# Pooled attention and a two-layer block on one core: the left-over keys of batch 0 used first, w1's first quarter in two loads, k of batch 1 and w2's second quarter ahead of q of batch 1

## The chip, the cores and the metric

The kernel runs on one core of one Trainium2 chip. The metric is the device time of one execution in microseconds (us), taken as the median of the runs. The core has five engines with a queue each: TensorE (PE, with its weight loads shown apart as PEld), VectorE (DVE), ScalarE (ACT), GpSimd (POOL) and SyncE (SP). Each queue runs in order, and DMAs are issued from SP's, ACT's and POOL's queues. A DMA issued from POOL can change the type of the data; here it turns float32 into 16 bits.

## What is computed

```python
batch, n_heads, seq, head_dim = (8, 8, 576, 64)      # q, k, v, float32
n_tokens, d_model, d_ff = (4608, 512, 2048)

k_p = k.reshape(B, H, 72, 8, D).mean(axis=3)         # keys and values averaged by eights
v_p = v.reshape(B, H, 72, 8, D).mean(axis=3)
scores = scale * q @ k_p^T
attn = exp(scores - max) / sum(exp(scores - max))
x = (attn @ v_p), heads side by side                 # 4608 x 512
h = x @ w_in                                         # w_in 512 x 2048, "w1" below
g = h - tanh(h)
out = g @ w_out                                      # w_out 2048 x 512, "w2" below
```

## The kernel before

The order of the work is written out by hand: within each engine's queue the instructions run in the order in which the code issues them, and semaphores that the framework derives from the tiles are all that holds one engine for another. The DMAs issued from POOL share eight semaphores in turn, so each of them also waits until the one eight places before it has landed; those of SP and ACT together share another eight in the same way.

**Batch by batch.** Batch b's 512 first query rows per head and its 64 last ones (the tail) are handled apart. Groups g = 0 to 8 are the two-layer block: groups 0 to 7 take the 512 first rows of a batch, group 8 collects all the tails. Group g's products run on PE while the other engines prepare batch g + 1. Group 0 is special: its output products (`mlp_o`, L625) go in four passes (quarters 0, 8, 4, 12 of w2's sixteen row blocks, `W2_ORDER`), for four blocks of 128 rows each; `mlp_o(0, tb, qd)` is row block tb with pass qd, four products of 512 columns. Later groups use a form with seven half products (L709) on sums and differences of w2's quarters, which `w_sum` (L695) builds into `w2s` during group 0 (`sum0` to `sum3`, `negated`).

**Tiles of keys.** The 8 heads have 72 pooled keys each, 576 rows. Two heads make 144 rows, of which 128 go into a main tile (four of them, t = 0 to 3) and 16 are left over; the left-overs of the four pairs (64 rows) make a fifth tile, NM. `load_main` loads main tiles, `load_dense` the left-over rows in one DMA, `load_left` in four. `pool_k` adds eights in three steps (8 to 4, 4 to 2, 2 to 1) and writes the result twice into `kd`; PE turns it (`turn_tile`); `kb_main` and `kb_left` copy it from PSUM into the layout `KB`. Scores of a main tile are one product of 512 columns, those of the left-overs four products on 32 rows each (`score_mms`), each followed by ACT's Exp. For batch 0, v is loaded as 16 bits into `v_bf` and pooled on PE with eight products (`v_pe_pool`, L900); the left-over v rows come as float32 and are cast by POOL (L862), and are then spread to their places by PE with the matrix `spread`. `v_main` and `v_left` multiply by a mask into `VB`. `av_pair` forms attn @ v with the sums in an extra column, divides (L954, L955) and `x0_turn` turns the result for `h_part`, the first products with w1 (L602).

**The start.** SP loads k of batch 0 (tiles 0, 1, then 2 and 3), ACT loads q of batch 0 in three parts, then the left-over keys and the left-over v rows. POOL makes the identity and the mask, loads v of batch 0, w1 in four quarters of 512 columns (`load_w1`, L783), w2's first quarter, casts the left-over v, loads q of batch 1 (tail L863, rest L864, in 16 bits, into unused parts of `w2s`), w2's second quarter, clears some tiles, loads v of batch 1 tiles 0 and 1 and w2's third quarter. SP's load of k of batch 1 (`load_k(1)`, L875) is tied to the landing of w1's second quarter. PE fills waits with `warm_pe`, products on zeros whose result is not used.

**Batch 1 in group 0.** `pool_k(1, nc.gpsimd, last=nc.vector)` (L1043) does the first addition on POOL (L268) and the other two on DVE, with `q1_reorder` (L254, two DVE copies from `q1_bf` to `q_bf`) between these. PE's order (L1044 to L1070): four blocks of `mlp_o` pass 0, q's transposes for head pairs 0 and 1, the keys' transposes, `mlp_o` block 0 of pass 1, the other q transposes and the tail, scores of tiles 0 and 1, block 1 of pass 1, the remaining scores, then five more blocks. Batch 2's loads on SP (L1072) are tied to the landing of w2's third quarter.

**PSUM.** Eight banks of 128 x 512 float32. `ps_any` hands them out: during batch 0's attention alternately from (5, 6, 7) and (0, 1, 2), later (`ps_b1`) in turn from (4, 5, 6, 7). The hidden tile i > 5 of group 0 uses bank i % 5; `mlp_o` blocks 0 to 3 collect in banks 1, 2, 3, 0.

Of the kernel before, what the change touches and what calls it, by code (L numbers as in the profile page):

```python
# [8 lines left out]
FP32 = mybir.dt.float32  # L9
# [20 lines left out]
NT = 5  # L30
# [4 lines left out]
NM = 4  # L35
# [8 lines left out]
def kernel(  # L44
# [9 lines left out]
    nc = tc.nc  # L54
# [28 lines left out]
    ps_h = Banks(0, 1, 2)  # L83
# [48 lines left out]
    q_raws = {}  # L132
    rot = [0]

    def ps_any(shape, dtype, name):
        pool, tag = [(ps_a, "ps_a"), (ps_h, "hT_ps")][rot[0] % 2]
        rot[0] += 1
        return pool.tile(shape, dtype, name=name, tag=tag)

# [9 lines left out]
    def load_main(src, dst, b, t0, t1, eng=nc.sync):  # L149
        return eng.dma_start(out=dst[:, t0:t1, :], in_=src[b, 0:128, t0:t1, :])  # L150
# [7 lines left out]
    def load_dense(src, dst, b, eng=nc.sync):  # L158
        return eng.dma_start(
            out=dst[0 : NM * LO, NM, :], in_=src[b, 128:PR, :, :]  # L160
        )
# [92 lines left out]
    def q1_reorder():  # L254
        for h in (0, 4):
            nc.vector.tensor_copy(
                out=q_bf[:, 0:R, h : h + 4, :].rearrange("p j h d -> p h j d"),
                in_=q1_bf[:, h : h + 4, :, :],
            )

    def pool_k(b, eng, t0=0, t1=NT, last=None, dep=None):
# [16 lines left out]
        )  # L278
        if b == 1:
            q1_reorder()  # L280
        kd_done = (last or eng).tensor_tensor(
# [495 lines left out]
    zeros = xT_last[:, 3, :, :].rearrange("p f c -> p (f c)")  # L777
    w1_dmas = []
    w2_dmas = []

    def load_w1(c):
        w1_dmas.append(
            nc.gpsimd.dma_start(  # L783
                out=w1b[:, :, c * 512 : (c + 1) * 512], in_=w1_src[:, :, c * 512 : (c + 1) * 512]
            )
        )

    def load_w2(i, n):
        w2_dmas.append(
            nc.gpsimd.dma_start(out=w2b[:, i : i + n, :], in_=w2_src[:, i : i + n, :])  # L790
        )
# [31 lines left out]
    load_q0(4, 8)  # L823
    load_dense(k_pairs, k_raw[0], 0, nc.scalar)
    load_dense(v_pairs, v_raw[1], 0, nc.scalar)
# [32 lines left out]
    )  # L858
    for c in range(4):
        load_w1(c)  # L860
    load_w2(0, 4)
    nc.gpsimd.tensor_copy(out=v_bf[:, NM, :], in_=v_raw[1][:, NM, :])  # L862
    nc.gpsimd.dma_start(out=q1_tail[:QT], in_=q[1, :, QA:S, :].rearrange("h p d -> p h d"))  # L863
    nc.gpsimd.dma_start(  # L864
        out=q1_bf, in_=q[1, :, 0:QA, :].rearrange("h (p j) d -> p h j d", j=R)
    )
    load_w2(8, 4)
    nc.gpsimd.memset(w2s[64:128, 3, 6:8, :], 0.0)
    nc.gpsimd.memset(k_raw[1][:, NM, :], 0.0)
    nc.gpsimd.memset(v_raw[0][:, NM, :], 0.0)  # L870
    nc.gpsimd.memset(KB[1][:, :], 0.0)
    load_main(v_pairs, v_raw[1], 1, 0, 2, nc.gpsimd)
    load_w2(4, 4)

    after(load_k(1), w1_dmas[1])  # L875

# [5 lines left out]

    def k_turn_left():
        ps = ps_any([128, 128], FP32, "kT_ps")
        turn_tile(ps[:, :], kdups[0], NM)
        kb_left(KB[0], ps, nc.vector.tensor_copy)

    pool_k(0, nc.vector, 0, 1)
# [34 lines left out]
    q_turn(nc.scalar.copy, 6, 8)  # L923
    pool_k(0, nc.vector, 2, 4)
    warm_pe(6)
    k_turn(2, 4)
    pool_k(0, nc.vector, NM, NT)
    warm_pe(2)
    q_pe_transpose(0, (2, 3), "act")
    vs0 = v_pe_pool(0, 2, ident, 4)  # L930
    v_main(VB[0], vs0, nc.vector, 0, 2)
    warm_pe(1, b0=3)
    scores_wide(0, (2, 3))
    v_ps = v_pe_pool(NM, NT, spread)
    k_turn_left()
    v_left(VB[0], v_ps[:, 0, :, :], nc.vector)
    warm_pe(1, b0=3)
    scores_wide(0, (NM,))
    vs1 = v_pe_pool(2, 4, ident, 3)
    v_main(VB[0], vs1, nc.vector, 2, 4)  # L940
    load_left(v_pairs, v_raw[1], 1, nc.scalar)
    pool_v1(NM, NT, nc.gpsimd)
    v1_last = load_main(v_pairs, v_raw[1], 1, 2, 4, nc.gpsimd)
    load_w2(12, 4)
    gts = []
# [38 lines left out]

    av_pair(0, 0, 1, (0, 1))
    av_pair(1, 0, 6, (0, 1))
    av_pair(0, 0, 1, (2,))
    av_pair(1, 0, 6, (2,))
    av_pair(0, 1, 3)
# [23 lines left out]
    for i in range(5, NHID):  # L1013
        mlp_h(0, i, gts, bank(i % 5 if i > 5 else 5, [128, TG]))
        if i == 7:
            q_pe_tail(0)
        if i == 9:
            scores_tail(0)
        if i == 11:
            ps_a.n = 0  # L1020
            av(0, 4, ps_any, True)
    def turn1(blk):
        x_pe_transpose(1, blk, x_pairs[1, blk // 2][:, blk % 2])
# [18 lines left out]

    pool_k(1, nc.gpsimd, last=nc.vector)  # L1043
    mlp_o(0, 0, 0, gts)  # L1044
    mlp_o(0, 1, 0, gts)
    mlp_o(0, 2, 0, gts)
    mlp_o(0, 3, 0, gts)
    q_pe_transpose(1, (0, 1), "act")
    k_transpose(1, ps_any, (nc.vector.tensor_copy, nc.vector.tensor_copy))
    sum1(0)  # L1050
    mlp_o(0, 0, 1, gts)
    q_pe_transpose(1, (2, 3), "act")
    q_pe_tail(1)
    sum2(0)
    sum0(0)
    pool_v1(0, 2)
    scores_wide(1, (0, 1))
    mlp_o(0, 1, 1, gts)
    scores_wide(1, (2, 3))
# [5 lines left out]
    sum0(4)  # L1065
    mlp_o(0, 2, 1, gts)
    mlp_o(0, 3, 1, gts)
    mlp_o(0, 0, 2, gts)
# [143 lines left out]
```

## Time and profile before

| | |
|---|---|
| median of 8 runs | 283.18 us (282.71 to 283.28) |
| the profiled execution | 283.22 us, its span 281.3 us |
| mean granted PE clock | 0.999 |
| DMA by queue (share of 16 engines' span) | SP 33.87 MB (47.9%), POOL 13.77 MB (19.9%), ACT 1.84 MB (2.2%) |
| first product with w1 (L602) | 16.27 us |
| first `mlp_o` (L631) | 31.54 us |
| first product of group 1 (L644) | 51.63 us |

The loads that matter here, from the view of DMA issues (start of the issue, us to landing):

| load | queue | issued | to landing |
|---|---|---|---|
| k batch 0 tiles 2, 3 (512 KB) | SP | 1.74 | 6.0 |
| left-over keys of batch 0 (128 KB) | ACT | 2.38 | 7.1 |
| left-over v of batch 0 (128 KB) | ACT | 3.07 | 7.2 |
| v batch 0 tiles 0, 1 (256 KB in 16 bits) | POOL | 3.70 | 7.0 |
| w1 first quarter (512 KB in 16 bits) | POOL | 5.96 | 9.2 |
| w1 fourth quarter | POOL | 8.17 | 18.3 |
| w2 first quarter | POOL | 8.90 | 21.2 |
| q tail of batch 1 | POOL | 11.27 | 19.3 |
| q of batch 1 | POOL | 11.97 | 21.3 |
| w2 second quarter | POOL | 12.85 | 23.2 |
| v batch 1 tiles 0, 1 | POOL | 15.73 | 21.6 |
| k batch 1 (1024 KB), then its left-overs | SP | about 18.4, 19.03 | 9.5, 9.8 |
| w2 third quarter | POOL | 18.83 | 21.0 |
| v batch 1 tiles 2, 3 | POOL | 22.49 | 18.6 |
| w2 fourth quarter | POOL | 26.72 | 16.8 |

The landings of w1's second and third quarter follow from the medians of neighbouring issues: about 18.5 and 21.9 us.

How to read the lines below: a line of a view in order of time has the start in us, the duration in us, the engine, the line of the code, the operation, what it writes and reads, and in brackets how long the engine was idle before and what released it. A line of the stretches has the stretch, its length, the busy us of PE, PEld, DVE, ACT and POOL (with the number of instructions), the granted PE clock, the share of the DMA engines and the GB/s. The durations of PE's products are modelled and overlap: a product of 512 columns shows 0.38 us, while twenty in a row take 4.31 us.

### The profile page before, as it was taken

Reading aid. Unit: us, or ns where it says so; the run is one execution under the profiler, and the core shown is the slowest. Engines: PE = TensorE matmul, PEld = TensorE weight load, DVE = VectorE, ACT = ScalarE, POOL = GpSimd, SP = SyncE. Lnnn points to the kernel's source line nnn. Section 1 sums busy time; section 2 is a strip of 40 time slices with the busy share of each in tenths; the row PEclk is TensorE's granted clock in tenths of the full one; section 3 lists DMA queues with packets and bytes.
Section 4 is the critical chain, followed back from the end, with each engine's and each line's share of the span. In section 5 each row is a group of like instructions: output and inputs, shape, how many; then the busy total and the mean of one; then the engine's idle time right before and its main releaser. Section 6 shows DMA issues by size and latency. Waiting matters only on the chain.

```text
span 281.3 us, 5492 instructions
## 1 busy us (share of the span) xinstructions
PE 273.6 (97%) x2172; PEld 180.8 (64%) x2174; DVE 221.5 (79%) x336; ACT 155.0 (55%) x209; POOL 116.4 (41%) x131
## 2 busy tenths in 40 slices
PE   7999999999999999999999999999999999999993
PEld 2574455446984598458845894589448954884683
DVE  6758988689948995799679976998599749927982
ACT  4757383777337734774376537662857156126510
POOL 8853401991695059604970398029901100010000
PEclk9999999999999999999999999999999999999999
DMA  7999999989858894879598969796730430021014
GB/s 246 241 212 277 229 261 349 250 178 304 222 99 228 255 274 80 222 248 293 91 193 252 321 88 153 233 349 116 161 117 1 86 149 2 0 89 64 0 41 111
DMA packets 66491, 49.82 MB, mean 177 GB/s; under 512 B 42104, under 2 KB 55944, under 8 KB 66466
## 3 DMA queue, kind: packets, MB, share of 16 engines
q1 hardware_dynamic: 55538, 33.87, 47.9%
q0 software_dynamic: 8736, 13.77, 19.9%
q10 hardware_dynamic: 2192, 1.84, 2.2%
q8 instruction: 17, 0.28, 0.5%
q14 instruction: 8, 0.07, 0.1%
HBM read 36.70 MB, written 9.44 MB: 164 GB/s over the span
## 4 chain that ended last, share of the span: by engine, by line
PE 85%; DMA 10%; DVE 1%; POOL 1%; SPq 0%; ACT 0%; issue 0%
PE PS L644 39%; PE PS L713 35%; DMA w2b<-in_moe_w_out_dram 8%; PE PS L631 4%; PE PS L483 3%; PE PS L457 3%; DMA k_raw<-in_k_dram 2%; PE PS L498 1%; PE PS L409 0%; PE PS L580 0%; POOL v_raw L862 0%; POOL w2s L864 0%; SPq L150 0%; DVE k_raw L268 0%; POOL w2s L863 0%; ACT qT L144 0%
## 5 line engine op out<-in xcount | busy, mean ns | idle before, releaser
L644 PE MATMUL PS<-xT,w1b 128*128 128x512 bf16 (+1 forms) x504 | 98.0, 355 | 0.0
L670 DVE TENSOR_TENSOR Gt<-PS,TS 128x1024 bf16<-128x1024 f32 x56 | 68.3, 1222 | 33.7 <-ACT TS L669 33.6
L644 PEld LDWEIGHTS <-w1b 128*128 128x128 f16 x576 | 56.3, 98 | 52.8
L669 ACT ACTIVATE TS<-PS 128x1024 f32<-128x1024 f32 x56 | 57.3, 1024 | 29.7 <-PE PS L644 27.4
L757 POOL TENSOR_TENSOR m<-O,m 128x512 f32<-128x512 f32 x6 | 7.6, 1259 | 75.1 <-ACT m L755 53.5
L713 PE MATMUL PS<-w2s,Dg 128*128 128x256 f16 x256 | 30.2, 273 | 0.0
L268 POOL TENSOR_TENSOR k_raw<-k_raw 128x512 f32<-128x512 f32 (+2 forms) x13 | 21.1, 1635 | 17.7 <-DVE w2s L696 16.3
L478 ACT ACTIVATE E<-PS 72x1024 bf16<-72x1024 f32 (+1 forms) x30 | 26.1, 929 | 3.9 <-PE PS L457 3.7
L713 PEld LDWEIGHTS <-Gt 128*128 128x128 bf16 x256 | 23.6, 98 | 6.9 <-issue 2.4
L713 PEld LDWEIGHTS <-P 128*128 128x128 bf16 x256 | 24.6, 98 | 3.0
L713 PEld LDWEIGHTS <-Dg 128*128 128x128 bf16 x256 | 24.6, 98 | 2.8
L678 DVE TENSOR_TENSOR P<-Gt 128x1024 bf16<-128x1024 bf16 (+1 forms) x31 | 22.0, 708 | 0.5
L764 ACT COPY m<-PS 128x512 f32<-128x512 f32 x8 | 4.7, 586 | 29.6 <-PE PS L713 29.6
L729 POOL DMA_DIRECT2D out_dram<-O x14 | 7.7, 553 | 31.6 <-DVE O L767 29.5
L688 DVE TENSOR_TENSOR Dg<-Gt 128x1024 bf16<-128x1024 bf16 x32 | 20.4, 685 | 0.0
L534 DVE TENSOR_TENSOR x_sb<-PS,rden 128x512 bf16<-128x512 f32 x28 | 19.4, 692 | 1.0
L293 POOL TENSOR_TENSOR v_raw<-v_raw 128x512 f32<-128x512 f32 (+1 forms) x12 | 18.7, 1575 | 0.0
L713 PE MATMUL PS<-w2s,Gt 128*128 128x256 f16 x128 | 16.4, 273 | 0.0
L713 PE MATMUL PS<-w2b,P 128*128 128x256 f16 x128 | 16.3, 273 | 0.0
L713 PE MATMUL PS<-w2b,Gt 128*128 128x256 f16 x128 | 16.3, 272 | 0.0
L713 PE MATMUL PS<-w2s,Q 128*128 128x256 f16 x128 | 16.3, 272 | 0.0
L1174 ACT COPY O<-PS 128x512 f32<-128x512 f32 x7 | 4.1, 585 | 21.9 <-PE PS L713 21.9
(124 smaller groups left out, 396.3 us busy)
## 6 DMA issues: line engine op xcount, KB each, us to landing
k_raw<-in_k_dram SPq DMA_DIRECT2D x7, 1024.0 KB, 6.0
out_dram<-O POOLq DMA_DIRECT2D x14, 512.0 KB, 4.7
v_raw<-in_v_dram SPq DMA_DIRECT2D x6, 1024.0 KB, 8.1
q_raw<-in_q_dram SPq DMA_DIRECT2D x6, 1024.0 KB, 11.3
w1b<-in_moe_w_in_dram POOLq DMA_DIRECT2D x4, 512.0 KB, 13.1
w2b<-in_moe_w_out_dram POOLq DMA_DIRECT2D x4, 512.0 KB, 21.1
v_raw<-in_v_dram POOLq DMA_DIRECT2D x2, 512.0 KB, 20.1
out_dram<-O SPq DMA_DIRECT2D x2, 512.0 KB, 6.5
```

Of the source, the lines that this page charges most:

```text
L268: first = eng.tensor_tensor(out=r[:, ta:tb, 0:4, :], in0=r[:, ta:tb, 0:4, :], in1=r[:, ta:tb, 4:8, :], op=ALU.add,)
L293: eng.tensor_tensor(out=r[:, ta:tb, 0:4, :], in0=r[:, ta:tb, 0:4, :], in1=r[:, ta:tb, 4:8, :], op=ALU.add,)
L457: nc.tensor.matmul(dst, lhsT=kv[a * D : (a + 1) * D, m, :], rhs=rhs, start=True, stop=True,)
L478: nc.scalar.activation(out=e, in_=ps, func=ACT.Exp, scale=SCALE)
L534: nc.vector.tensor_tensor(out=x_sb[:, :, :, :], in0=ps[:, :, :, 0:D], in1=rden[:, :, :, :].to_broadcast([128, 2, 4, D]), op=ALU.mult,)
L631: nc.tensor.matmul(o_ps[:, :], lhsT=gts[i][:, tb * 128 : (tb + 1) * 128], rhs=w2b[:, i, :], start=(i == 0), stop=(i == NHID - 1),)
L644: nc.tensor.matmul(dst[:, t0 * 128 : t1 * 128], lhsT=w1b[:, fb, i * 128 : (i + 1) * 128], rhs=x[:, t0:t1, fb, :], start=(fb == 0), stop=(f ...
L669: nc.scalar.activation(out=t2, in_=PS[:, b0 : b0 + 2, :], func=ACT.Tanh)
L670: nc.vector.tensor_sub(out=Gt[:, p, :, :], in0=PS[:, b0 : b0 + 2, :], in1=t2)
L678: nc.vector.tensor_tensor(out=P[:, a:b, :], in0=Gt[:, a:b, 0, :], in1=Gt[:, a:b, 1, :], op=ALU.add)
L688: return nc.vector.tensor_tensor(out=Dg[:, a:b, :, :], in0=Gt[:, a:b, :, 0:HT], in1=Gt[:, a:b, :, HT:TG], op=ALU.subtract,)
L713: nc.tensor.matmul(part(g, bk, tt), lhsT=lhs(k, slice(tt * 128, (tt + 1) * 128)), rhs=rhs[:, k, :], start=(first and k == 0 and (tt == 0 o ...
```

## The change

- The left-over keys of batch 0 are loaded on SP behind the main tiles, not on ACT. They are pooled, turned (`k_turn_left(3)`) and scored ahead of tiles 2 and 3. Their warm-up product goes, the banks of batch 0's attention are written out, and `av_pair` takes its three parts in one go.
- w1's first quarter is loaded as two halves of 256 columns.
- k of batch 1 is loaded from POOL's queue, behind w1, not from SP's with a tie. Behind it come w2's first and second quarter, then q of batch 1; then the batch 1 left-over v (its four small loads are issued by SP, not ACT), v tiles 0 and 1, w2's third quarter, and, inside the loop over hidden tiles (before tile 15 is issued), batch 1's `pool_k`, v tiles 2 and 3 and w2's fourth quarter.
- In batch 1 the keys' transposes come ahead of the fourth block of pass 0; `sum1(0)` and `q1_reorder` follow, two blocks of pass 1, all q transposes, and the scores lie between the last two blocks of pass 1.

```diff
@@ pool_k
-        if b == 1:
-            q1_reorder()
@@
-    def load_w1(c):
...
+    def load_w1(c0, c1):
+        nc.gpsimd.dma_start(out=w1b[:, :, c0:c1], in_=w1_src[:, :, c0:c1])
@@
-    load_dense(k_pairs, k_raw[0], 0, nc.scalar)
+    load_dense(k_pairs, k_raw[0], 0)
     load_dense(v_pairs, v_raw[1], 0, nc.scalar)
@@
-    for c in range(4):
-        load_w1(c)
+    for c0, c1 in ((0, 256), (256, 512), (512, 1024), (1024, 1536), (1536, 2048)):
+        load_w1(c0, c1)
+    load_main(k_pairs, k_raw[1], 1, 0, NM, nc.gpsimd)
+    nc.gpsimd.tensor_copy(out=v_bf[:, NM, :], in_=v_raw[1][:, NM, :])
+    nc.gpsimd.memset(k_raw[1][:, NM, :], 0.0)
+    load_dense(k_pairs, k_raw[1], 1, nc.gpsimd)
     load_w2(0, 4)
-    nc.gpsimd.tensor_copy(out=v_bf[:, NM, :], in_=v_raw[1][:, NM, :])
+    nc.gpsimd.memset(w2s[64:128, 3, 6:8, :], 0.0)
+    load_w2(8, 4)
     nc.gpsimd.dma_start(out=q1_tail[:QT], in_=q[1, :, QA:S, :].rearrange("h p d -> p h d"))
+    nc.gpsimd.memset(v_raw[0][:, NM, :], 0.0)
+    nc.gpsimd.memset(KB[1][:, :], 0.0)
     nc.gpsimd.dma_start(
         out=q1_bf, in_=q[1, :, 0:QA, :].rearrange("h (p j) d -> p h j d", j=R)
     )
-    load_w2(8, 4)
...
-    load_main(v_pairs, v_raw[1], 1, 0, 2, nc.gpsimd)
-    load_w2(4, 4)
-
-    after(load_k(1), w1_dmas[1])
@@
+    banks = iter((5, 0, 6, 1, 7, 2, 5, 0, 6, 1, 0, 5))
+
+    def ps_any(shape, dtype, name):
+        return bank(next(banks), shape)
@@
     pool_k(0, nc.vector, 2, 4)
+    pool_k(0, nc.vector, NM, NT)
     warm_pe(6)
     k_turn(2, 4)
-    pool_k(0, nc.vector, NM, NT)
     warm_pe(2)
     q_pe_transpose(0, (2, 3), "act")
+    k_turn_left(3)
     vs0 = v_pe_pool(0, 2, ident, 4)
     v_main(VB[0], vs0, nc.vector, 0, 2)
-    warm_pe(1, b0=3)
-    scores_wide(0, (2, 3))
-    v_ps = v_pe_pool(NM, NT, spread)
-    k_turn_left()
+    v_ps = v_pe_pool(NM, NT, spread, 2)
     v_left(VB[0], v_ps[:, 0, :, :], nc.vector)
-    warm_pe(1, b0=3)
-    scores_wide(0, (NM,))
+    warm_pe(1, b0=7)
+    scores_wide(0, (NM, 2, 3))
     vs1 = v_pe_pool(2, 4, ident, 3)
     v_main(VB[0], vs1, nc.vector, 2, 4)
-    load_left(v_pairs, v_raw[1], 1, nc.scalar)
+    ps_a.n = 7
+    load_left(v_pairs, v_raw[1], 1)
     pool_v1(NM, NT, nc.gpsimd)
-    v1_last = load_main(v_pairs, v_raw[1], 1, 2, 4, nc.gpsimd)
-    load_w2(12, 4)
+    load_main(v_pairs, v_raw[1], 1, 0, 2, nc.gpsimd)
+    load_w2(4, 4)
@@
-    av_pair(0, 0, 1, (0, 1))
-    av_pair(1, 0, 6, (0, 1))
-    av_pair(0, 0, 1, (2,))
-    av_pair(1, 0, 6, (2,))
+    av_pair(0, 0, 1)
+    av_pair(1, 0, 6)
@@ the loop over hidden tiles
+        if i == 14:
+            pool_k(1, nc.gpsimd, last=nc.vector)
+            load_main(v_pairs, v_raw[1], 1, 2, 4, nc.gpsimd)
+            load_w2(12, 4)
@@
-    pool_k(1, nc.gpsimd, last=nc.vector)
     mlp_o(0, 0, 0, gts)
     mlp_o(0, 1, 0, gts)
     mlp_o(0, 2, 0, gts)
+    k_transpose(1, ps_any, (nc.vector.tensor_copy, nc.vector.tensor_copy))
     mlp_o(0, 3, 0, gts)
+    sum1(0)
+    q1_reorder()
+    mlp_o(0, 0, 1, gts)
+    mlp_o(0, 1, 1, gts)
     q_pe_transpose(1, (0, 1), "act")
-    k_transpose(1, ps_any, (nc.vector.tensor_copy, nc.vector.tensor_copy))
-    sum1(0)
-    mlp_o(0, 0, 1, gts)
     q_pe_transpose(1, (2, 3), "act")
     q_pe_tail(1)
...
+    mlp_o(0, 2, 1, gts)
     scores_wide(1, (0, 1))
-    mlp_o(0, 1, 1, gts)
+    mlp_o(0, 3, 1, gts)
     scores_wide(1, (2, 3))
...
-    mlp_o(0, 2, 1, gts)
-    mlp_o(0, 3, 1, gts)
```

More of the change, by code (lines that the diff above doesn't have):

```diff
@@ L132 @@
     q_raws = {}
[L133 to L138, printed above, removed]
     evac_n = [0]
@@ L777 @@
     zeros = xT_last[:, 3, :, :].rearrange("p f c -> p (f c)")
-    w1_dmas = []
     w2_dmas = []
-    def load_w1(c):
[L782 to L786, printed above, removed]
+    def load_w1(c0, c1):
+        nc.gpsimd.dma_start(out=w1b[:, :, c0:c1], in_=w1_src[:, :, c0:c1])
     def load_w2(i, n):
@@ L866 @@
     )
-    load_w2(8, 4)
[L868 to L871, printed above, removed]
-    load_main(v_pairs, v_raw[1], 1, 0, 2, nc.gpsimd)
-    load_w2(4, 4)
-    after(load_k(1), w1_dmas[1])
     def k_turn(ta, tb):
@@ L881, in k_turn, with k_turn_left @@
         kb_main(KB[0], ps, ta, tb, (nc.vector.tensor_copy, nc.vector.tensor_copy))
-    def k_turn_left():
-        ps = ps_any([128, 128], FP32, "kT_ps")
+    def k_turn_left(b0):
+        ps = bank(b0, [128, 128])
         turn_tile(ps[:, :], kdups[0], NM)
         kb_left(KB[0], ps, nc.vector.tensor_copy)
+    banks = iter((5, 0, 6, 1, 7, 2, 5, 0, 6, 1, 0, 5))
+    def ps_any(shape, dtype, name):
+        return bank(next(banks), shape)
     pool_k(0, nc.vector, 0, 1)
```

## The prediction

> **What bounds the kernel now.** I read the page first (busy time, then the chain that ended last), then busy time in stretches of 5 us, then PE, DVE and POOL in order of time from 9 to 19 us, then the chain between 30 and 46 us, last each DMA with its time to landing.
>
> ```profile
> PE 273.6 (97%) x2172; PEld 180.8 (64%) x2174; DVE 221.5 (79%) x336; ACT 155.0 (55%) x209; POOL 116.4 (41%) x131
> ...
> PE 85%; DMA 10%; DVE 1%; POOL 1%; SPq 0%; ACT 0%; issue 0%
> ```
>
> PE is busy 273.6 of 281.3 us: it sets the time, and only PE's gaps and what lies ahead of them can be won. The stretches (us, then PE, PEld, DVE, ACT, POOL busy) say where they are:
>
> ```profile
> 10.00:15.00 5.00, 4.58 (x60) 3.20 (x59) 3.95 (x11) 2.76 (x5) 4.46 (x7) 1.00 1.22 199
> 15.00:20.00 5.00, 4.70 (x53) 4.21 (x55) 2.56 (x7) 3.10 (x6) 2.20 (x4) 1.00 1.24 217
> ...
> 35.00:40.00 5.00, 4.66 (x47) 2.61 (x45) 4.22 (x10) 3.68 (x8) 0.00 (x0) 1.00 1.17 277
> ```
>
> The 5 us stretches from 20 to 35 us, and every one from 40 to 250 us, show PE full. So a shift of the point where PE becomes dense (about 16.3 us), and a gap closed at 35 to 40 us, pass to the end one for one. Batch 0's attention, in order of time (start, us, engine, line):
>
> ```profile
> 10.44 0.89 POOL L862 CAST v_raw<-v_raw 128x512 bf16<-128x512 f32 x1 [0.75 <-DVE KB L354]
> ...
> 12.29 0.23 DVE L357 CAST KB<-PS 64x64 bf16<-64x64 f32 x1
> ...
> 12.57 0.40 PE L409 MATMUL PS<-qT,KB 128*32 128x512 bf16 x4
> ...
> 12.90 0.62 PE L900 MATMUL PS<-v_raw,ident 128*128 128x128 bf16 x8
> ...
> 13.56 0.43 DVE L334 TENSOR_TENSOR VB<-PS,mask 128x256 bf16<-128x256 f32 x1 [0.59 <-PE PS L900]
> ...
> 14.21 0.21 DVE L954 RECIPROCAL rden<-PS 128x8 f32<-128x8 f32 x1 [0.22 <-PE PS L498]
> ```
>
> The left-over scores (12.57) wait for the left-over keys' copy (L357, done 12.52). Their exp (ACT 13.03 to 13.63) then holds the last part of the attention product, hence L954 at 14.21; from there four normalisations at 0.85 us, a transpose and ACT's copy lead to the first h product at 16.27. In the chain of 30 to 46 us:
>
> ```profile
> 12.85 23.22 DMA w2b<-in_moe_w_out_dram
> 36.07 0.04 issue
> 36.11 1.02 PE PS L631 x4
> ...
> 37.40 0.59 ACT qT L144
> 37.99 0.04 issue
> 38.03 0.38 PE PS L409
> ```
>
> PE has two gaps here. It waits for w2's second quarter, landed at 36.07 (0.23 us shown idle). The second score tile of batch 1 starts at 38.03, when ACT has emptied the PSUM bank that it takes; a 512-column product issues every 0.2155 us (20 L631 in 4.31), so the first one, begun at 37.54, was through at 37.76: 0.27 us, hidden in the modelled durations.
>
> **The change part by part.** (1) *Batch 0, PE.* One warm-up product goes (0.22 us). PE's order is now: left-over keys turned, both pools of v (L900), left-over scores, scores 2 and 3. DVE pools the left-over keys ahead of the copies of KB for tiles 2 and 3: 9.47, 9.92, 10.25, end 10.54 (0.43, 0.29, 0.29 as at 3.77 to 4.56); KB copies then end 11.16 instead of 10.40, the left-over copy (0.23) 11.42. That needs the left-over keys by 9.47. Their load moves from ACT's queue (issued 2.38, 7.1 us) behind SP's 512 KB (issued 1.74, 6.0 us, landed 7.8): 128 KB more, about 8.5. PE then waits for POOL's cast of the left-over v. POOL has five w1 issues and batch 1's k ahead of it: 5.96 + 6 x 0.75 (2.99 us for four) = 10.46, as late as before (10.44); end 11.35. So: L900 on spread 11.41 (0.23), warm-up 0.22, left-over scores 11.86 (0.33), two scores 12.2 (0.43), L900 12.65, L334 (0.66 after it) 13.3 to 13.73, L954 13.74 instead of 14.21. **Front: -0.47.** Covers: scores 2 and 3 now end their exps about 14.0, where the second half's product wants them at 13.8; four normalisations at 0.85 us cover that. The first product needs w1's columns 0 to 255 at 15.8; the whole quarter landed at 15.2. Bounds: the longest POOL issue (0.94) for all six gives a cast end of 12.5, +1.1 on this sum; a cast without wait would win 0.2 more.
>
> (2) *w1 in two loads.* The same bytes in 512 B packets, for 1 KB. The 31 to 33 us stretch is q of batch 1 in 512 B packets (205 GB/s), 18.8 to 21.5 is w1 in 1 KB packets (205 GB/s): nothing on the engines. One more issue (0.75) is counted in (1).
>
> (3) *ACT* loses five issues (0.66 and 1.77 us): nothing, since its next copies wait for q at 5.85 and for PE at 15.20. *SP* takes them (left v from 11.4 instead of 13.1); nothing waits behind them until batch 2's loads, held for w2's third quarter, 39.9. The last stores wait on the same relative predecessors.
>
> (4) *POOL's queue.* Landed before (issue plus landing): w1 15.2, 18.5, 21.9, 26.5; k of batch 1 by SP 28.9; w2 first quarter 30.1; q tail 30.6; q 33.3; w2 second 36.07; v 37.3; w2 third 39.8; v 41.1; w2 fourth 43.5. As built, each POOL load waits for the eighth before it: w2 second for w1's first half, q's tail for the other, q for w1's second quarter (18.5), v for the third, w2 third for the fourth. All are issued over 10 us ahead of their turn. From w1's second quarter on, the new order by rows: 512 KB as f16 take 2.6 us (0.55 MB in 18.8 to 21.5), so w1 ends at 23.8; k 1.15 MB at 325 GB/s (37.5 to 39.5) 27.3; w2 first 29.9; second 32.5; q tail 33.0; q (2.7) 35.7. By order alone: the same transfers as before stand ahead of q's end, so 36.07. I take 36.07. Bounds: issued 18.6, plus the shortest landing of a w2 load (16.8) 35.4, plus q's own (21.3) 39.9.
>
> (5) *Batch 1 on PE.* PE enters the output products (31.54) at 31.07; w2 first has 1 us in hand. Three blocks (12 x 0.2155) end at 33.66. Keys: POOL adds 27.4 to 30.3 (2.9), DVE's two adds (0.82 each) come after the 15th h tile, 31.76 to 33.4: in time. The 16th tile (0.69) ends 34.12; the fourth block takes its bank, PE would be there at 34.10: **+0.08**. The 0.23 gap for w2 second is gone: **-0.23**. Two more blocks end at 36.76; q's reorder, first half, is ready at 36.07 + 0.06 + 0.42 + 0.06 = 36.61: **0**, with 0.15 in hand; any more lateness stalls PE in full (+3.7 at 39.9, nothing won at 35.4). Transposes end 37.66; the tail's bank is emptied by ACT at 37.84: **+0.18**. A block now lies between transposes and scores, so the 0.27 bank gap goes: **-0.27**. The attention product at 43.7 needs v (DVE done 43.05, since v lands unchanged): covered by 0.6.
>
> Sum: -0.47 + 0.08 - 0.23 + 0 + 0.18 - 0.27 = **-0.71**, against this execution's 283.22 (span 281.3 and 1.9 around it): 282.5. The median of the runs is 283.18, 0.04 below; same number.
>
> A rule against this change: k leaves a hardware queue for POOL's. Row: POOL's issues at 8.17 and 8.90 lie beside DVE adds with two SBUF inputs (7.82 to 9.43) and take 0.78 and 0.79, against 0.75 for one of the four alone. The added k issue lies beside the same kind of adds (9.47 to 10.54), so I keep 0.75. The Trainium skill (SBUF — State Buffer, "SBUF: two separate sides" and "A bandwidth-pool intuition that's wrong") says that a DVE operation in a two-port mode locks GpSimd out, so that it can't write the descriptors of its DMAs, and 620 ns became about 3100 ns. Were these adds such operations, the k issue would take about 3.1 instead of 0.75 and an estimate by that page would be 2.35 us above the forecast, 284.9; the row shows no such stretching, and it decides.
>
> **The rivals.** *q lands late (slower).* q of batch 1 is now last of five loads wanted before 37 us, with 0.15 us of slack. If it takes as long as its tail did (19.3), it lands 37.9: stall 1.7, total 284.2. It decides from a landing of 36.9 (gain spent), and is measurable from 37.5. For: w2 second, last in the old order, was still landing at 36.07 while v's f32 already moved at over 350 GB/s from 34.3, so single engines trail. Against: the old order had the same trail, and is in the 36.07.
>
> *The front does not move (same).* If POOL's issues grow (0.85 each), the cast ends 11.95 and the front gives nothing: 283.1. For: 0.89 for q's issue. Against: five issues took 3.73. A q landing near 36.7 ends there too.
>
> *More front (faster).* If the cast waits less and exps pack tighter, -0.3 more: 282.2. Then q's landing binds, which caps it.
>
> *It does not do what it says.* If the left-over keys land after 9.5, KB for tiles 2 and 3 waits too; at 10.2 (old landing 9.48 plus 0.7) the cast still covers all but 0.1. No case of its own.
>
> **How the numbers follow.** Forecast 0.48 (282.2 to 282.9), q late 0.23 (283.8 to 286.2), front unmoved or q half late 0.21 (282.8 to 283.8), more front 0.08. A measurement of this kernel tells 0.2% (0.57 us) from none. Faster: 0.40 of the forecast and 0.07 of the last; slower: q late and 0.02 of the unmoved; the rest same: 0.47, 0.28, 0.25. The range 281.9 to 284.3 leaves out the upper part of q late and little below.
>
> **What would show it.** L954's first reciprocal near 13.74; POOL's cast near 10.46; k landed by 28.9 with POOL's add done by 31.9; no PE idle before the second w2 quarter; q's reorder starting at 36.1 without a wait of PE on q_bf longer than 0.2; the second score tile right behind the first; PE's first L644 near 50.9 (51.63 before). A PE wait at 36 to 38 us on the reorder, or L954 later than 14, makes the prediction wrong.

## The result, and the profile after

| | before | after |
|---|---|---|
| median | 283.18 us (28 runs) | 282.12 us (10 runs, 281.82 to 282.36) |
| ratio after/before | | 0.9963, 95% interval 0.9955 to 0.9971 |
| profiled execution, its span | 283.22, 281.3 | 282.21, 280.2 |
| ACT begins to cast q's third part | 8.84 | 9.83 |
| first reciprocal | 14.21 | 14.14 |
| first product with w1 | 16.27 | 16.20 |
| first output product of group 0 | 31.54 | 31.47 |
| first product of group 1 | 51.63 | 51.08 |
| end of the last DVE copy | 277.39 | 276.84 |
| from there to the end of the span | 3.87 | 3.36 |

The change makes the kernel 1.06 us (0.4%) faster. In the profiles the gain has three places: 0.07 us ahead of the first product with w1, 0.48 between that product and group 1, nothing from there to the last copy, and 0.51 behind the last copy. Line numbers of the code after are 6 to 13 lower than before: L954 is now L943, L631 L623, L644 L636, L409 L401, L891 L881, L862 L849, L900 L890.

The page of the kernel after, busy time and the shares of the chain that ended last:

```profile
PE 273.5 (98%) x2172; PEld 180.6 (64%) x2173; DVE 221.3 (79%) x336; ACT 155.1 (55%) x209; POOL 118.4 (42%) x134
...
PE 95%; DMA 3%; ACT 0%; ACTq 0%; DVE 0%; issue 0%
```

PE is busy as long as before; what went is idle time around it. Its stretches of 5 us:

```profile
10.00:15.00 5.00, 4.73 (x62) 3.17 (x61) 3.50 (x12) 3.62 (x7) 3.94 (x7) 1.00 1.34 193
15.00:20.00 5.00, 4.99 (x55) 4.28 (x55) 2.49 (x7) 3.17 (x6) 1.89 (x4) 1.00 1.25 218
...
35.00:40.00 5.00, 5.00 (x39) 2.81 (x38) 4.87 (x12) 2.62 (x6) 0.00 (x0) 1.00 1.17 270
```

The stretch of 35 to 40 us, in which PE had been busy 4.66 us, is full. Between 10 and 15 us PE still has gaps. PE of the kernel after, in order of time:

```profile
34.80 2.32 PE L623 MATMUL PS<-w2b,Gt 128*128 128x512 f16 x10
36.96 1.06 PE L222 MATMUL PS<-ident,q_bf 128*128 128x128 bf16 x16
38.02 0.28 PE L234 MATMUL PS<-ident,w2s 128*128 128x64 bf16 x4
38.13 1.03 PE L623 MATMUL PS<-w2b,Gt 128*128 128x512 f16 x4
39.00 0.59 PE L401 MATMUL PS<-qT,KB 128*128 128x512 bf16 x2
...
51.08 0.59 PE L636 MATMUL PS<-xT,w1b 128*128 128x512 bf16 x2
```

No line has a bracket, so PE waits for nothing here. Two score tiles (L401) stand in one line of 0.59 us: the second follows the first directly. At the front, ACT, POOL, DVE and PE in order of time:

```profile
9.83 1.14 ACT L881 CAST q_bf<-q_raw 128x512 bf16<-128x512 f32 x2 [0.96 <-DMA q_raw<-in_q_dram]
...
10.75 0.61 POOL L849 CAST v_raw<-v_raw 128x512 bf16<-128x512 f32 x1 [0.40 <-DMA v_raw<-in_v_dram]
...
11.52 0.23 DVE L349 CAST KB<-PS 64x64 bf16<-64x64 f32 x1
...
12.30 0.94 PE L401 MATMUL PS<-qT,KB 128*32 128x512 bf16 x6
...
14.14 0.21 DVE L943 RECIPROCAL rden<-PS 128x8 f32<-128x8 f32 x1
```

The copy of the left-over keys (L349) ends 0.77 us earlier than before, at 11.75. But ACT now waits 0.96 us for q's third part, which it had at 8.84 before, and the scores, all six products in one line, begin at 12.30. The chain that ended last, followed through this stretch, names q's load (start, us, what):

```profile
1.84 7.96 DMA q_raw<-in_q_dram
...
9.83 1.15 ACT q_bf L881 x2
...
11.48 0.68 PE PS L890 x16
...
12.30 0.94 PE PS L401 x6
```

### The profile page after: what moved, and what is told of

Read it like the earlier page. It is cut to its first block, busy times and chain, and to the rows that moved or that the text cites. A ratio compares the mean times of both kernels' runs of the same rounds, so it can differ in the third digit from the quotient of the medians.

```text
span 280.2 us, 5491 instructions
## 1 busy us (share of the span) xinstructions
PE 273.5 (98%) x2172; PEld 180.6 (64%) x2173; DVE 221.3 (79%) x336; ACT 155.1 (55%) x209; POOL 118.4 (42%) x134
## 4 chain that ended last, share of the span: by engine, by line
PE 95%; DMA 3%; ACT 0%; ACTq 0%; DVE 0%; issue 0%
PE PS L636 39%; PE PS L705 35%; PE PS L594 5%; PE PS L623 5%; DMA q_raw<-in_q_dram 3%; PE PS L475 3%; PE PS L449 3%; PE PS L490 1%; PE PS L401 1%; PE PS L222 0%; ACT q_bf L881 0%; PE PS L572 0%; PE PS L890 0%; PE PS L956 0%; ACTq L797 0%; PE PS L790 0%
## 5 line engine op out<-in xcount | busy, mean ns | idle before, releaser
L636 PE MATMUL PS<-xT,w1b 128*128 128x512 bf16 (+1 forms) x504 | 98.0, 355 | 0.0
L636 PEld LDWEIGHTS <-w1b 128*128 128x128 f16 x576 | 56.4, 98 | 52.8
L705 PE MATMUL PS<-w2s,Dg 128*128 128x256 f16 x256 | 30.2, 272 | 0.0
```

The costliest lines, as they stand in the source:

```text
L636: nc.tensor.matmul(dst[:, t0 * 128 : t1 * 128], lhsT=w1b[:, fb, i * 128 : (i + 1) * 128], rhs=x[:, t0:t1, fb, :], start=(fb == 0), stop=(f ...
L705: nc.tensor.matmul(part(g, bk, tt), lhsT=lhs(k, slice(tt * 128, (tt + 1) * 128)), rhs=rhs[:, k, :], start=(first and k == 0 and (tt == 0 o ...
```

## The experiments

All kernels compute the whole result. In the table, "front" is the first reciprocal, "batch 1" the time from the first product with w1 to the first product of group 1, "tail" the time from the end of the last copy to the end of the span; these and the cast of q's third part are from one profile each. Intervals are of the ratio to the kernel before.

| kernel | median us | ratio, 95% | q cast | front | batch 1 | tail |
|---|---|---|---|---|---|---|
| before | 283.18 | | 8.84 | 14.21 | 35.36 | 3.87 |
| after | 282.12 | 0.9963 (0.9955 to 0.9971) | 9.83 | 14.14 | 34.88 | 3.36 |
| after_again | 281.98 | 0.9958 (0.9945 to 0.9971) | 9.82 | 14.13 | 34.87 | 3.31 |
| keys_act | 282.22 | 0.9966 (0.9953 to 0.9978) | 9.67 | 14.52 | 34.88 | 3.38 |
| keys_act_2 | 282.13 | 0.9959 (0.9944 to 0.9974) | 8.88 | 13.56 | 34.94 | 3.39 |
| front_old | 282.49 | 0.9972 (0.9961 to 0.9983) | 9.09 | 14.40 | 34.87 | 3.29 |
| order_old | 282.89 | 0.9992 (0.9981 to 1.0004) | 9.83 | 14.76 | 34.87 | 3.48 |
| b1_old | 283.09 | 0.9997 (0.9988 to 1.0005) | 10.17 | 14.56 | 35.15 | 3.74 |
| q_first | 282.91 | 0.9989 (0.9980 to 0.9998) | 9.79 | 14.10 | 35.68 | 3.41 |
| scores_early | 282.64 | 0.9984 (0.9973 to 0.9994) | 9.55 | 13.86 | 35.52 | 3.30 |
| w1_whole | 282.06 | 0.9961 (0.9948 to 0.9973) | 9.82 | 14.13 | 34.88 | 3.39 |
| q_split | 282.46 | 0.9972 (0.9960 to 0.9983) | 9.54, 10.65 | 14.44 | 34.88 | 3.45 |
| after_plus2 | 282.66 | 0.9982 (0.9973 to 0.9991) | 9.71 | 14.03 | 34.88 | 3.78 |
| before_plus6 | 282.81 | 0.9990 (0.9981 to 0.9999) | 9.00 | 14.33 | 35.20 | 3.48 |

**The change once more (after_again).** The kernel unchanged, beside the next ones.

> The changed kernel once more, unchanged. In the two profiles PE's end moved by 0.55 us but the span by 1.06: 0.5 lie behind the last copy (3.87 us to the span's end before, 3.36 after). If that is chance of one execution, this profile's end is anywhere from 3.3 to 3.9 while its first product of group 1 stays at 51.0 to 51.2; if the change itself shortens the end, it is again 3.3 to 3.4. Time 282.1.

281.98 us, and the profile repeats every point of the table within 0.07 us. Not every landing is repeated: the second load of k of batch 0 is added up from 7.89, 0.28 us earlier.

**The left-over keys' load back on ACT (keys_act).**

```diff
-    load_dense(k_pairs, k_raw[0], 0)
+    load_dense(k_pairs, k_raw[0], 0, nc.scalar)
```

> The changed kernel with batch 0's left-over keys loaded on ACT's queue again, behind q; all else as changed. Theory (shared transfers): on SP these keys ran at the same time as q's third part (heads 4 to 7) and made that land at 9.8 instead of 8.8 us, which held the q casts and so the whole front. On ACT, q's third part lands by 8.9 and the cast starts by 9.1 (9.83 in the changed kernel), the keys land near 9.5, the first reciprocal of batch 0 comes at 13.7 to 13.9 (14.14), and the time is 0.2 to 0.4 us below the changed kernel: 281.7 to 281.9. Rival (the late q was this one execution's, or POOL's cast at 10.75 sets the front): the first reciprocal stays at 14.0 to 14.2 and the time within 0.1 of 282.1.

282.22 us, no gain, and the six times lie in two groups: 281.73 to 281.89, and 282.54 to 282.95. The profile, of an execution of 282.54, has q's cast at 9.67 and the keys pooled only from 10.16, both behind a load; the first reciprocal is at 14.52. One profile of a kernel with two groups decides nothing, so it was run again at the end (keys_act_2).

**The front of the kernel before, with the new batch 1 (front_old).** Batch 0's attention and the left-over keys' queue as before; all loads from w1 on, and batch 1, as after.

```diff
-    load_dense(k_pairs, k_raw[0], 0)
+    load_dense(k_pairs, k_raw[0], 0, nc.scalar)
@@
-    pool_k(0, nc.vector, NM, NT)
     warm_pe(6)
     k_turn(2, 4)
+    pool_k(0, nc.vector, NM, NT)
...
+    warm_pe(1, b0=3)
+    scores_wide(0, (2, 3))
...
-    warm_pe(1, b0=7)
-    scores_wide(0, (NM, 2, 3))
+    warm_pe(1, b0=3)
+    scores_wide(0, (NM,))
```

> The changed kernel with batch 0's attention as before (order, banks, keys on ACT), keeping the new loads and the new order of batch 1. Theory: the front gave 0.07 us and batch 1's gaps about 0.5, so this is 282.1 to 282.3, with the first output product (L623 there, 31.47) at 31.5 to 31.6 and PE's first product of group 1 near 51.1. Rival (the front is worth the 0.47 of the forecast): 282.5 to 282.6.

282.49 us: without the new front 0.7 us of the gain is still there. Its front is at 14.40 against 14.14. So the new front is worth 0.3 us in the profiles and 0.4 to 0.5 in the medians, though the profiles of before and after show only 0.07. One pair of profiles is not enough here: the three kernels with the old front and the keys on ACT have their first reciprocal at 14.21, 14.33 and 14.40.

**The new front with the batch 1 of before (b1_old).** k of batch 1 on SP tied to w1's second quarter, POOL's old order, the left-over v of batch 1 on ACT, PE's old order in batch 1.

```diff
-    load_main(k_pairs, k_raw[1], 1, 0, NM, nc.gpsimd)
+    load_w2(0, 4)
...
-    load_w2(0, 4)
...
-    load_w2(8, 4)
...
+    load_w2(8, 4)
...
+    load_main(v_pairs, v_raw[1], 1, 0, 2, nc.gpsimd)
+    load_w2(4, 4)
+
+    after(load_k(1), w1_dmas[2])
@@
-    load_left(v_pairs, v_raw[1], 1)
+    load_left(v_pairs, v_raw[1], 1, nc.scalar)
```

> The changed front of batch 0 and w1 in two halves, but k of batch 1 on SP, the old order of POOL's loads and the old order of batch 1. Theory: the gap at w2's second quarter (0.23) and the gap between the two score tiles (0.27) are back, so 283.0 to 283.2, PE's first product of group 1 at 51.5 to 51.6. Rival (the gain lies in the front, or in the last stores whatever batch 1 does): 282.1 to 282.6.

283.09 us: the whole gain is gone, more than batch 1 alone holds. The profile is 0.27 us longer in batch 1, 0.42 at the front (q's cast at 10.17) and 0.38 behind the last copy. The 0.42 comes with late landings in this execution (the second load of k of batch 0 is added up from 8.71, from 8.17 in the profile after); PE and DVE have the order of the changed kernel there. Of the two gaps in batch 1 one came back in this profile: the two score tiles take 0.87 us again, but PE comes to the output products at 31.88 (31.54 in the kernel before), and no wait is shown when it uses w2's second quarter at 36.25. The 0.38 belongs to no term of the forecast, and led to the next two.

**Where the last stores stand among the shared semaphores (after_plus2, before_plus6).** The change issues two DMAs fewer on SP and ACT (both loads of k of batch 1 go to POOL), so every later DMA of SP and ACT, the last stores too, stands two places earlier among the eight that these share. Counted by order of issue, the very last store moves from place 1 to place 7. Splitting two loads of q of late batches in halves puts it back; splitting six in the kernel before moves it to 7.

```diff
-        nc.sync.dma_start(
-            out=t[:, :, 0:R, :], in_=q[b, :, 0:QA, :].rearrange("h (p j) d -> p h j d", j=R)
-        )
+        for h0, h1 in ((0, 4), (4, 8)) if b >= 6 else ((0, 8),):
+            nc.sync.dma_start(
+                out=t[:, h0:h1, 0:R, :],
+                in_=q[b, h0:h1, 0:QA, :].rearrange("h (p j) d -> p h j d", j=R),
+            )
```

For before_plus6 the same edit in the kernel before, with `b >= 2`.

> The changed kernel with the loads of q of batches 6 and 7 in two halves each: two more DMAs on SP in the steady part, so the eight semaphores that SP's and ACT's DMAs share in turn stand at the end as in the kernel before (the last store waits for, and then uses, number 1, not number 7). Theory (the place of the last stores among the eight sets how long the program's end takes): from the last copy's end to the span's end 3.8 to 3.9 us (3.36 and 3.3 in the changed kernel's two profiles), PE's end unmoved, time 282.5 to 282.6. Rival (the end got shorter for another reason, such as what the transfers of the last group do): 3.3 to 3.4, time 282.1.

> The kernel before with the loads of q of batches 2 to 7 in two halves each: six more DMAs on SP, which sets the eight semaphores at the end as in the changed kernel (the last store on number 7). Nothing of the change itself is in it. Theory: from the last copy's end to the span's end 3.3 to 3.4 us instead of 3.87, PE's products as before (first product of group 1 at 51.6), time 282.6 to 282.8. Rival: end 3.8 to 3.9, time 283.2.

With two DMAs more, the changed kernel is at 282.66, 0.6 us slower than its other runs, though its front is 0.1 earlier. The kernel before, with nothing of the change in it, is 0.35 us faster with six more. The tail is 3.78 and 3.48. Over all fourteen profiles, the eleven whose last store has place 7 have tails of 3.29 to 3.48, the three with place 1 have 3.74 to 3.87. The stretches (length, busy us of five engines, clock, DMA share, GB/s) at the end of before, after and after_plus2:

```profile
278.89:279.39 0.50, 0.00 (x0) 0.00 (x0) 0.00 (x0) 0.00 (x0) 0.00 (x0) 1.00 0.69 201
279.39:279.89 0.50, 0.00 (x0) 0.00 (x0) 0.00 (x0) 0.00 (x0) 0.00 (x0) 1.00 0.00 0
...
280.89:281.26 0.37, 0.00 (x0) 0.00 (x0) 0.00 (x0) 0.00 (x0) 0.00 (x0) 0.50 0.00 0
```

```profile
278.34:278.84 0.50, 0.00 (x0) 0.00 (x0) 0.00 (x0) 0.00 (x0) 0.00 (x0) 1.00 0.60 176
278.84:279.34 0.50, 0.00 (x0) 0.00 (x0) 0.00 (x0) 0.00 (x0) 0.00 (x0) 1.00 0.00 0
...
279.84:280.20 0.36, 0.00 (x0) 0.00 (x0) 0.00 (x0) 0.00 (x0) 0.00 (x0) 1.00 0.00 0
```

```profile
278.24:278.74 0.50, 0.00 (x0) 0.00 (x0) 0.00 (x0) 0.00 (x0) 0.00 (x0) 1.00 0.62 180
278.74:279.24 0.50, 0.00 (x0) 0.00 (x0) 0.00 (x0) 0.00 (x0) 0.00 (x0) 1.00 0.00 0
...
280.24:280.50 0.26, 0.00 (x0) 0.00 (x0) 0.00 (x0) 0.00 (x0) 0.00 (x0) 1.00 0.00 0
```

By these stretches the last bytes move until about 2.0 us behind the last copy in all three (279.39 less 277.39, 278.84 less 276.84, 278.74 less 276.74). What differs lies behind that: 1.87, 1.36 and 1.76 us with no engine and no transfer at work. SP's queue shows what part of it is. At the end of the program SP waits for the eight shared semaphores one after the other, always in the same order; where nothing holds it, it takes 0.06 us for each. The lines below are the waits that it still has ahead of it when the last store has landed (number, ns of one, us of the first and the last start) before, after, in after_plus2 and in before_plus6:

```profile
L1207 SPq EVENT_SEMAPHORE  x8: 27/28/28, 279.9 to 280.4; - x8
```

```profile
L1199 SPq EVENT_SEMAPHORE  x2: 28/28/28, 279.2 to 279.3; - x2
```

```profile
L1201 SPq EVENT_SEMAPHORE  x8: 28/28/28, 279.2 to 279.6; - x8
```

```profile
L1209 SPq EVENT_SEMAPHORE  x2: 28/28/28, 279.9 to 279.9; - x2
```

With place 1, SP stands at the first of the eight until the last store lands, and then has all eight to go through: 0.51 us from that landing to the end of the row, in all three profiles. With place 7 it has gone through six of them while the store was under way: 0.14 us, in one profile of the eleven 0.18. What follows the row takes 0.84 to 0.85 us, in q_split 0.97. So 0.37 of the 0.51 us is a shorter end of the program, and the place of the last store among the eight sets it. The other 0.13 is the last store's own landing, 2.51 us behind the last copy before and 2.38 after; the fourteen profiles scatter from 2.31 to 2.51 there. The median of before_plus6 moved by about these 0.37 us. Of the 0.6 us of after_plus2 its profile shows 0.30; where the rest lies is not shown.

**w1's first quarter in one load (w1_whole).**

```diff
-    for c0, c1 in ((0, 256), (256, 512), (512, 1024), (1024, 1536), (1536, 2048)):
+    for c0, c1 in ((0, 512), (512, 1024), (1024, 1536), (1536, 2048)):
```

> The changed kernel with w1's first quarter in one load again. The forecast put the split at one more issue (0.75) and nothing on the transfers. Theory (the cast of the left-over v waits for that load's landing, 10.75, and q's third part sets the front): no change, 282.0 to 282.2, the first h product at 16.1 to 16.3. Rival (the split, or the issue it adds, costs the front): first reciprocal at 13.7 to 13.9, time 281.7 to 281.8; other way: if the first h products wait for w1, 282.3 or more.

282.06 us, every point of the table within 0.07 us of the changed kernel's. The two halves show no effect.

**q of batch 1 ahead of w2's second quarter again (q_first).**

```diff
     load_w2(0, 4)
...
-    load_w2(8, 4)
...
     nc.gpsimd.dma_start(
         out=q1_bf, in_=q[1, :, 0:QA, :].rearrange("h (p j) d -> p h j d", j=R)
     )
+    load_w2(8, 4)
```

> The changed kernel with q of batch 1 loaded ahead of w2's second quarter, as before the change. Theory (the two take the same place in the queue in turn, so the one that is last lands at 36.0): q lands near 33.4, w2's second quarter near 36.0; PE, which ends pass 0 at 35.2, waits 0.8 for it; time 282.8 to 283.0. Rival (the order of these two does not matter, the bank gap alone gave the gain): within 0.2 of 282.1.

282.91 us, +0.8 against the changed kernel's runs, and batch 1 takes 0.80 us more. PE in order of time:

```profile
35.99 1.89 PE L623 MATMUL PS<-w2b,Gt 128*128 128x512 f16 x8 [0.63 <-DMA w2b<-in_moe_w_out_dram]
37.72 1.06 PE L222 MATMUL PS<-ident,q_bf 128*128 128x128 bf16 x16
```

PE waits for w2's second quarter, which lands at 36 us as the last of the five, and q's transposes begin 0.76 us later (37.72 for 36.96). So PE's new order needs the new order on POOL; the new loads with PE's old order were not run.

**Scores directly behind the transposes (scores_early).**

```diff
+    scores_wide(1, (0, 1))
     mlp_o(0, 2, 1, gts)
-    scores_wide(1, (0, 1))
```

> The changed kernel with batch 1's first two score tiles right behind q's transposes, ahead of the third block of pass 1, as near to the old order as the new one allows. Theory (a score tile waits for ACT to empty its PSUM bank, which the block between covers): PE stands still for 0.4 to 0.9 us between 38.2 and 39.2, the first product of group 1 comes at 51.5 to 51.9 and the time is 282.5 to 282.9. Rival (the waiting was chance, or the covering block only moves it): 282.0 to 282.2.

282.64 us, +0.5. Its front came out 0.28 us earlier than the changed kernel's by itself (q's cast at 9.55), and batch 1 is 0.64 us longer. PE in order of time:

```profile
37.73 0.28 PE L234 MATMUL PS<-ident,w2s 128*128 128x64 bf16 x4
38.22 0.87 PE L401 MATMUL PS<-qT,KB 128*128 128x512 bf16 x2 [0.21 <-ACT qT L138]
38.92 1.24 PE L623 MATMUL PS<-w2b,Gt 128*128 128x512 f16 x5
```

Both parts of the wait are to be seen: 0.21 us ahead of the first score tile, in the bracket, and then two tiles that take 0.87 us, where they take 0.59 when the second follows directly. The starts give the whole of it: the first score tile comes 0.49 us behind the tail's products (the block that stands there in the changed kernel comes after 0.11), and the next block 0.70 behind the score tile (0.43 there): 0.38 and 0.27 us more, together 0.65.

**The order at the front alone (order_old).** front_old, with the left-over keys on SP as in the changed kernel. So the old front (PE's and DVE's order, the PSUM banks, one more warm-up product, and `av_pair` in parts) is all that parts it from the changed kernel.

```diff
-    load_dense(k_pairs, k_raw[0], 0, nc.scalar)
+    load_dense(k_pairs, k_raw[0], 0)
```

> Batch 0's attention in the old order and banks, but with the left-over keys on SP; new loads and new batch 1. Against the changed kernel it differs in the order alone. Theory (the order is worth what the forecast gave it, 0.47, and the keys on SP cost it again, by landing q's third part at 9.7 to 9.8): first reciprocal at 14.5 to 14.8 (14.13 in the changed kernel), first h product at 16.6 to 16.9, time 282.5 to 282.7. Rival (the order is worth little, and the late q costs nothing): first reciprocal at 14.1 to 14.3, time 282.0 to 282.3.

282.89 us, 0.8 above the changed kernel's runs; q's cast starts at the same 9.83. ACT, DVE and PE in order of time:

```profile
9.83 1.14 ACT L882 CAST q_bf<-q_raw 128x512 bf16<-128x512 f32 x2 [0.97 <-DMA q_raw<-in_q_dram]
...
10.93 0.63 DVE L268 TENSOR_TENSOR k_raw<-k_raw 128x256 f32<-128x256 f32 x1
...
12.84 0.23 DVE L355 CAST KB<-PS 64x64 bf16<-64x64 f32 x1 [0.16 <-PE PS L361]
...
14.76 0.21 DVE L945 RECIPROCAL rden<-PS 128x8 f32<-128x8 f32 x1 [0.22 <-PE PS L496]
```

The left-over keys are added up behind the copies of KB and copied at 12.84 (11.52 in the changed kernel); the first reciprocal is at 14.76, not 14.14. At equal starts of q's cast the order, with its banks, is worth 0.62 us. And in the old order, moving the keys to SP costs 0.4 us (282.49 to 282.89).

**q's third part in two loads (q_split).** Two loads of two heads each, the left-over v on SP, and later loads split so that the last stores keep their place.

```diff
-    load_q0(4, 8)
+    load_q0(4, 6)
+    load_q0(6, 8)
@@
-    load_dense(v_pairs, v_raw[1], 0, nc.scalar)
+    load_dense(v_pairs, v_raw[1], 0)
```

> The changed kernel with q's third part (heads 4 to 7 of batch 0) in two loads of two heads on ACT, and the left-over v on SP behind the left-over keys; seven later DMAs (q of batches 2 to 7, one q tail) are split too, which leaves the eight shared semaphores as they are at the end. Theory (q's third part sets the front): the first of the two lands at 8.7 to 9.2, so its cast starts by 9.3 (9.82), the first reciprocal comes at 13.8 to 14.0 (14.13), and the time is 281.7 to 282.0. Rival (v of batch 0, landing at 11.1 on POOL's queue, sets the front as much): reciprocal at 14.1, time 282.1.

282.46 us, slower. The first half is cast from 9.54, 0.3 us sooner, but the second only from 10.65, where in one load both are cast in the 1.14 us from 9.83 on; the first reciprocal is at 14.44.

**The left-over keys on ACT, again (keys_act_2).** The kernel of keys_act.

> The left-over keys on ACT's queue again, as in keys_act, whose times fell into two groups (281.7 to 281.9, and 282.5 to 283.0) and whose profile came from the slower one, with the keys pooled from 10.16 on. Theory: the two groups differ by how early the left-over keys, now last on ACT's queue but one, and q's third part land; a profile of the faster group shows q's cast by 9.3, the keys pooled from 9.5 to 9.7 and the first reciprocal at 13.7 to 13.9, one of the slower group is like the first. Rival: the groups have nothing to do with the front, and the first reciprocal is at 14.4 to 14.6 again at a time of 281.9 or less.

282.13 us (281.53 to 282.38, seven runs, on another chip than keys_act), again in a wide band and again no better than the changed kernel. The profile is of the fastest one:

```profile
8.88 1.14 ACT L881 CAST q_bf<-q_raw 128x512 bf16<-128x512 f32 x2 [0.35 <-DMA q_raw<-in_q_dram]
...
9.53 0.42 DVE L262 TENSOR_TENSOR k_raw<-k_raw 128x256 f32<-128x256 f32 x1 [0.25 <-DMA k_raw<-in_k_dram]
...
13.56 0.21 DVE L943 RECIPROCAL rden<-PS 128x8 f32<-128x8 f32 x1
...
15.63 0.82 PE L594 MATMUL PS<-xT,w1b 128*128 128x256 bf16 x6
```

With q at 8.88 and the keys at 9.53, the landings that the forecast reckoned with, the new order gives the first reciprocal at 13.56, 0.65 before the old kernel's. When the same loads land later, as in keys_act (9.67 and 10.16), it gives 14.52. No kernel tried beats the changed one by more than its measurement is uncertain.

## Why the prediction was right or wrong

The direction and the range were right; the time was 0.4 us too long (282.5, measured 282.12, which is 0.08 below the 282.2 to 282.9 of the forecast's own case). One of the signs that it named against itself came: the first reciprocal is later than 14, at 14.14. Of the sum of -0.71, the profiles show -0.07 - 0.48 = -0.55, and -0.51 came from a place that the forecast had at nothing.

**Batch 1: the two gaps right, the two costs not.** The terms come to -0.24, -0.50 for the gaps and +0.26 for the costs; measured -0.48. The wait for w2's second quarter (-0.23) and the bank wait ahead of the second score tile (-0.27) are both gone, and q_first and scores_early bring each back alone, at 0.80 and 0.64 us, which is more than before: in PE's new order pass 1 follows pass 0 directly, and ACT has all four of q's copies to make when the scores come. The two costs did not come: the keys' adds on DVE were done at 33.72, the fourth block followed the transposes at 34.37 without a wait (0 for +0.08), and the sixteen transposes of q took 1.06 us, so the tail's products at 38.02 and the block at 38.13 found their banks free (0 for +0.18). The price of -0.23 holds for the old front alone. In b1_old and before_plus6 PE comes to the output products 0.34 and 0.12 us later, and batch 1 takes 35.15 and 35.20 us instead of 35.36: part of the wait is spent. So "one for one" holds for a shift at the front only where no landing binds behind it; in the old batch 1 an earlier PE would have waited longer for w2 (argued, not run).

**The landings of POOL's loads: right.**

| | k batch 1 | w2 first | w2 second | q tail | q | v | w2 third | w2 fourth |
|---|---|---|---|---|---|---|---|---|
| forecast | 27.3 | 29.9 | 32.5 | 33.0 | 35.7 / 36.07 | 37.3 | 39.8 | 43.5 |
| measured | 27.45 | 30.2 | 32.7 | 33.1 | 35.96 | 37.3 | 39.6 | 43.45 |

The rule that the sum of bytes ahead of a load sets its landing, whatever their order, held within 0.3 us. PE came to q's transposes at 36.96, 0.35 us behind the 36.61 at which the forecast had the first half of the reorder ready; so the rival of a late q did not come, and q_first shows what the same 36 us cost when PE wants that place sooner.

**The issue of k on POOL: right.** It took 0.80 us (9.55 to 10.35), beside DVE adds with two SBUF inputs (9.36 to 10.44), for 0.75 reckoned. The Trainium skill's rule (SBUF — State Buffer, "A bandwidth-pool intuition that's wrong") that a DMA of a locked-out GpSimd takes about five times as long is not what this row shows; the page states it for a DVE copy in a two-port mode, and no run was made with such a copy beside an issue.

**The front: the order right, the landing wrong.** The forecast was -0.47, the measurement -0.07. The step that failed is the one that priced the move of the left-over keys by their own landing alone ("128 KB more, about 8.5") and took q's as given. The keys were in time (added up at 9.70 with no wait). POOL's cast started 0.29 us late for another reason than reckoned, a wait for the left-over v, and took 0.61 for 0.89 us, so it ended at 11.36, as forecast (11.35). What failed is q's third part: its 512 KB landed 8.0 us after their issue (7.0 before), and ACT could cast them at 9.83, not at 8.84. The queues' shares between 6 and 8 us (packets, MB, share of 16 engines; q10 is ACT's, q1 SP's) in the kernel before, then in the one after:

```profile
q10 hardware_dynamic: 474, 0.49, 72.4%
q1 hardware_dynamic: 138, 0.25, 34.6%
```

```profile
q1 hardware_dynamic: 218, 0.39, 54.4%
q10 hardware_dynamic: 314, 0.32, 50.8%
```

SP's queue has 0.14 MB more to move in these 2 us, the left-over keys' 128 KB, and ACT's queue, with q, moves 0.17 MB less. On ACT's queue the keys stood behind q; on SP's they run beside it. front_old and order_old, which differ in this one load, show the same (ACT's queue 76.7 and 49.9%). The Trainium skill (DMA: Bandwidth & Descriptors, "Queues, rings and completion order") states that each DMA engine takes packets from all queues with work in turn; the even shares with the keys on SP (54.4 and 50.8%) agree.

Not all of the 0.99 us is this. The second load of k, on SP ahead of the keys, was also 0.35 us later in the profile after (added up from 8.17, from 7.82 before), and such a shift of all early loads comes and goes from one execution to the next. Counted from that addition, q's cast starts 1.0 to 1.3 us later in the five profiles with the keys on ACT, and 1.5 to 1.9 later in the eight with the keys on SP and q in one load. The two groups do not meet, and their means lie 0.6 us apart: that is what the move costs q.

In the runs of the new order with the keys on SP whose q came in one load, the first reciprocal is q's cast plus 4.31 to 4.32 us (9.55 and 13.86, 9.71 and 14.03, 9.83 and 14.14); b1_old, with 10.17 and 14.56, is at 4.39. So there q's landing sets the front. order_old shows that the order is worth 0.62 us where the forecast had 0.47, and the profiles of before and order_old (14.21 and 14.76, with the same order at the front) that the later landing costs 0.55 there, 0.36 against front_old (14.40).

What stays open: putting the keys back on ACT, which should give q's landing back, did not shorten the median in two sets of runs. The two profiles show that the early loads of that kernel land up to 0.8 us apart from one execution to the next (q 8.88 and 9.67, the keys 9.53 and 10.16; the two ran on two chips, but front_old and keys_act, with the same early loads on one chip, have q at 9.09 and 9.67), and that the keys then bind as well as q. What decides which of them comes was not found.

**The end: not foreseen.** The forecast named the right thing and drew the wrong conclusion: "the last stores wait on the same relative predecessors" does not price what two DMAs fewer do to the place of the last store among the shared semaphores. SP has two waits left instead of eight when that store lands, 0.37 us less, and after_plus2 and before_plus6 move this in both directions; the other 0.13 of the 0.51 is within the scatter of that landing. The front's shortfall of 0.40 was hidden in the sum by the end's unforeseen 0.51 and by the 0.24 that batch 1 gave beyond its terms. That the time came within 0.4 us is luck to that extent.

**w1 in halves: right**, at nothing.

## What to carry to other kernels

A load that moves from one queue to another is priced by what it then runs beside, not only by its own landing: here 128 KB in parallel to a 512 KB load made that one land about 0.6 us later, which took back more than half of what a 0.6 us better order had won. The loads of POOL's queue landed by the sum of the bytes ahead of them, so an order for them should follow the order in which PE wants them, and PE's order is to be changed with it. When a change adds or removes DMAs, compare the time behind the last transfer too, or 0.4 us is credited to the wrong edit.

## What the runs showed of the hardware

The end of a program is not a constant. Between the landing of the last store and the end of SP's waits for the shared semaphores lie 0.14 us in the changed kernel and 0.51 in the one before, and two loads split in halves, which change nothing at the end but the count of DMAs, make it 0.51 again: SP goes through its eight waits in a fixed order, and what counts is how many stand behind the last store's. And the first ten microseconds scatter: with the same early loads, q's third part was cast from 8.88 in one profile and from 9.67 in another (two chips), and from 9.09 and 9.67 in two profiles of one chip. One pair of profiles doesn't price an edit at that place.
